# Step 1's first conv block added in pairs, and step 0's second product with two copies and two subtractions in other places

## The chip, the core and the metric

The kernel runs on one NeuronCore of a Trainium2 chip. The metric is the device time of one execution in microseconds; the number to compare is the median of several runs. The engines have their own instruction queues and meet by semaphores: TensorE (PE in the profile) multiplies, VectorE (DVE), ScalarE (ACT) and GpSimd (POOL) work on tiles in SBUF and PSUM, and SyncE (SP) issues transfers. GpSimd issues transfers as well, among them those that add to their destination (accumulates).

## The reference

`x` has 8 batches of 4096 positions with 192 channels; the channels form 8 heads with 7 weights each.

```python
w = exp(weight - max(weight))              # per head, over the 7 taps
w = w / (sum(w) + 1e-9)
x_pad = 6 rows of zeros in front of x
conv[b, s, channel] = sum over k of w[head, k] * x_pad[b, s + k, channel]

x = conv.reshape(32768, 192)
h = x @ w_in                               # 192 x 2048
g = h * (1.0 / (1.0 + np.exp(-1.702 * h)))
out = g @ w_out                            # 2048 x 192
```

Everything is float32.

## The kernel before, in words

The 32768 positions are worked in 32 steps (`N_BIG`, numbered from 0). A step takes a stretch of positions of two parts (n = 0, 1), has the convolution in three blocks of channels (c = 0, 1, 2), multiplies by `w_in` (the first product, line 599), applies the activation (ScalarE, lines 616 and 621), and multiplies by `w_out` (the second product, line 1045; in step 0 lines 845 and 850). Both products use schemes that replace some block products by sums of blocks. VectorE and GpSimd form those sums (`add_up`, lines 360 and 362). VectorE and ScalarE combine the product terms in PSUM banks (`sum2`, line 640; `copy2`, line 634).

Nothing reorders the instructions: each engine runs its queue in the order in which the program lists them. The steps from 2 on follow one list. Steps 0 and 1 are special, because step 0's weights and inputs are just arriving. The order around the change is written out in `first_step`, and in the generator `second_first`, which holds step 0's second product. That product works with two-by-two blocks: weights a11 to a22, activations b11 to b22, sums s1 to s4 and t1, t2, each in two halves [0] and [1]. The products go to four PSUM banks: `c11`, `a`, `c12`, `c21`. `go` issues matmuls in the rows 0 to 95 of a bank (line 845), and beside each group one that belongs to another bank's rest (`side`, line 850), whose result ScalarE copies away (line 852).

The bank `a` is used for three sums in a row, a11·b11, then + s2·t2, then + s3·b12, and each intermediate value is copied or added elsewhere before the next matmuls add to the bank. Line 890 copies the first value to `p1`, line 903 the second into the bank `c12`, and line 909 the second, later value into `c21`. Line 883 forms t2[1] = b22 − t1[1]; lines 906 and 913 later overwrite t2[0] and t2[1] with b21 − t2, which the product into `c21` uses. The values leave the banks by additions (907, 915, 943) and by transposes (961).

While step 0's second product runs, step 1's convolution is finished. Block c = 1 is made by VectorE (lines 474 and 476, `conv`). Blocks c = 2 and c = 0 are made by taps: ScalarE multiplies by one weight each (line 490, `tap`), the first into the block's own place, the other six into separate places, and the seven are added by accumulating transfers which GpSimd issues (line 513, `add_taps`). The list `TREE_1` gives the order of these additions: (1,2), (3,4), (0,1), (5,6), (0,3), (0,5), where (a,b) adds tap b to tap a. Each transfer moves 128 x 512 elements, 256 KB.

When all seven taps of c = 0 are in place and VectorE's convs are done, `need("done 1")` makes the first block sum (`OPEN_SUM`, the first L360 behind the convs). Behind it come the transfers that copy blocks between the halves of the partitions (`cross`, line 527), the other block sums (`next_sum`), the sums of `w_in` for the later scheme (`next_w`), and step 1's first product. In GpSimd's queue the accumulates are followed by the transfers of `add_forms` (line 409), whose other copies are on ScalarE (405 and 407).

Results of the first product are kept in PSUM banks and in places in SBUF called rooms (`room`); `ROOM_OF` says which value k0 to k9 goes to which room.

Of the kernel before, what the change touches and what calls it, by code (L numbers as in the profile page):

```python
# [15 lines left out]
def kernel(  # L16
# [289 lines left out]
    def split_piece(i, part=slice(0, PIECE)):  # L306

        split_e(i, part)
        split_m(i, part)

# [71 lines left out]
    def round_w_out(i):  # L382
        join_piece(NW + i)
        sign_piece(NW + i)
# [15 lines left out]
        round_piece(NW + i, dsts)  # L400
# [83 lines left out]
    TREE_1 = {2: [(1, 2)], 4: [(3, 4), (0, 1)], 6: [(5, 6), (0, 3), (0, 5)]}  # L484

    def tap(big, c, k):
# [11 lines left out]
        for a, b in (TREE if big > 1 else TREE_1).get(k, ()):  # L498
            tree.append((homes[a], homes[b]))
# [10 lines left out]
    def add_taps():  # L510
        if tree:
            out, src = tree.pop(0)
            nc.gpsimd.dma_start(out=out, in_=src, accum_op=ALU.add)  # L513

# [132 lines left out]
    FIRST = [  # L647
# [12 lines left out]
    ]  # L660
    ROOM_OF = ((4, 0, 3, 2, 1, 1, 0, 1, 1, 2), (0, 1, 4, 2, 3, 3, 2, 3, 3, 2))

    FILL = [
        {
            0: (("tap",), ("tap",), ("tap",), ("tap",), ("add", 4)), 2: (("add", 4), ("turn", 0)), 12: (("add", 4),),
            16: (("turn", 1),), 40: (("turn", 2),),
        },
        {
            0: (("vsum",),), 4: (("g", 0),), 7: (("vsum",), ("vsum",), ("vsum",), ("vsum",)), 10: (("vsum",),),
            13: (("g", 1),), 15: (("g", 2),), 17: (("g", 3),), 18: (("vsum",),), 20: (("vsum",),), 22: (("vsum",),),  # L670
            26: (("g", 4),), 32: (("vsum",),), 40: (("cross",),), 42: (("cross",),),
        },
    ]
    FILL_1 = [
        {
            0: (("tap",),), 3: (("add", 12), ("tap",), ("work", 0.8)), 4: (("work", 0.8),), 13: (("work", 0.8),),
            15: (("work", 0.8),), 16: (("tap",),), 23: (("tap",),), 31: (("tap",),),
        },
        {
            4: (("form", 2),), 5: (("g", 0), ("work", 0.8)), 9: (("g", 1),), 10: (("work", 0.8),),  # L680
            11: (("form", 3),), 14: (("turn", 0),), 17: (("turn", 1),), 19: (("turn", 2),), 20: (("g", 2),),
            25: (("g", 3),), 31: (("work", 0.8),), 32: (("g", 4), ("forms",)),
        },
    ]

    COUNT = {}
    for item in FIRST:
        for name in {s for s in item[2:] if isinstance(s, str) and s[0] == "a"}:
# [6 lines left out]
    def do(big, v, half, kind, *args):  # L695
# [7 lines left out]
        def at(name):  # L703
            return where[name] if name[0] == "a" else rooms[ROOM_OF[v][int(name[1:])]]
# [22 lines left out]
    later = []  # L727

    def seeds_ahead(big, half):

        while later and later[0][0] == "copy":
            dst = later[0][1]
            if dst[0] == "a" and dst not in half[0] and not free:
                return
            do(big, 0, half, *later.pop(0))

    def rest_ahead(big, half):
        while later:
            do(big, 0, half, *later.pop(0))

    def plain(u, m, n, v, slot, ks=range(NC), first=0):

        for k in ks:
            product1(slot, NC * (2 * u + m) + k, 2 * k + n, 0, v, k == first)

    def fill(big, kind, *args):
        if kind == "work":
            work(*args)
# [11 lines left out]
        elif kind == "form":  # L760
            add_forms(*args)
        elif kind == "turn":
# [8 lines left out]
    def hidden(big, v, now, nxt):  # L771

        for i, (ahead, *item) in enumerate(FIRST):
            for what in (FILL if big > 1 else FILL_1)[v].get(i, ()):
                fill(big, *what)
            if not ahead:
                do(big, v, now, *item)
            elif v == 0:
                do(big, 1, nxt, *item)
            elif nxt and ahead == 2:  # L780
                do(big + 1, 0, nxt, *item)
            elif nxt:
                later.append(item)
# [3 lines left out]

    def second_first(between, fetch, last_seeds):

        n3 = NC * Q  # L790
        groups = ((0, 2), (3, 1))

        def four(t, pi):
            return t.rearrange("p (v q h) e -> p v q h e", v=2, h=2)[:, :, pi, :, :]

        def place4(t):
            return t.rearrange("p (v h e) -> p v h e", v=2, h=2)

        pairs = g.rearrange("p (v q) n o (s h) t -> p v q n o s (h t)", v=2, s=2)

        def rows4(n, pi):
            return pairs[:, :, pi // 2, n, :, pi % 2, :]

        ws = [w_out_s[:, m, :, :] for m in range(2)]
        a11, a12, a21, a22 = ([four(t, pi[j]) for pi in groups] for t in ws for j in range(2))
        b11, b12, b21, b22 = ([rows4(n, pi[j]) for pi in groups] for j in range(2) for n in range(2))
        w4, t4 = NG * HD, NG * TOK
        room0 = conv_t[:, AT_X + NV - 5 : AT_X + NV, :].rearrange("p b t -> p (b t)")
        old0 = own(0).rearrange("p b t -> p (b t)")
        t1 = [place4(flat_room[:, 0:t4]), place4(places[:, 0:t4])]  # L810
        t2 = [place4(flat_room[:, t4 : 2 * t4]), place4(osbs)]
        s1, s2, s3, s4 = (
            [place4(flat[:, i * w4 : (i + 1) * w4]) for flat, i in two]
            for two in (
                ((flat_form, FORMS - 2), (old0, 0)), ((flat_form, FORMS - 1), (old0, 1)),
                ((room0, 0), (old0, 2)), ((old0, 3), (room0, 1)),
            )
        )
        p5, q12 = (flat_room[0:n3, 2 * t4 + i * TOK : 2 * t4 + (i + 1) * TOK] for i in range(2))
        p1 = room0[0:n3, 3 * T : 3 * T + TOK]  # L820
        assert 2 * w4 <= 3 * T and 4 * w4 <= NBLK * T and t4 <= (NA - 4 * NC) * UW
        add, sub = vec.tensor_add, vec.tensor_sub
        js = slice(0, TOK // Q)

        c11, a, c12, c21 = (slots[i][h] for h in range(2) for i in range(2))
        side = []

        def listed(w, t, gs=(0, 1)):
            return [
                (w[i][:, v, h, :], t[i][:, v, :, h * T : (h + 1) * T])  # L830
                for i in gs for v in range(2) for h in range(2)
            ]

        def aside(banks, *stages):

            for steps, to, start in stages:
                for c, bank in enumerate(banks):
                    for i, (w, t) in enumerate(steps):
                        last = to is not None and i == len(steps) - 1
                        side.append((bank[n3:, :], w[:, chunk_cols(c)], t, start and i == 0, last and chunk(to, c)))  # L840

        def go(bank, steps, first=True, more=False):
            for i, (w, t) in enumerate(steps):
# [553 lines left out]
```

## Time and profile before

| | us |
|---|---|
| three runs | 2267.24, 2268.92, 2269.05 |
| median | 2268.92 |
| profiled execution: span | 2266.2 |
| its time with TensorE busy | 2248.7 |
| with VectorE busy | 1981.8 |
| with ScalarE busy | 1708.1 |
| with GpSimd busy | 1067.6 |

The profile describes one execution on the core; for this one its span is the time that is known, and the runs' median stands 2.7 us above it. The steps from 2 on take the bulk of the span; the changed part lies between about 60 and 108 us from the start of the span, where the second product of step 0 and the first of step 1 meet. In the views a row gives the start, the busy time, the engine, the line of the kernel, the operation, what it writes and reads, the shape and the number of instructions taken together (x4). A bracket at the end gives the idle time in front of it and what ended it. The rows of stretches give for each engine the busy time and the number of instructions, then the granted TensorE clock, the share of the DMA engines, and GB/s.

### The profile page before, as it was taken

To read this page: it belongs to the slowest core of one execution; us is meant where nothing else is said; L and a number is where in the kernel's file an instruction comes from. 1 tells how busy PE (TensorE), PEld (TensorE's weight loads), DVE (VectorE), ACT (ScalarE), POOL (GpSimd) and SP (SyncE) were. 2 spreads that over 40 slices of the span, in tenths; PEclk is the share of its full clock that TensorE was granted. 3 is DMA by queue.
4 is the path that set the end of the run, shared out by engine and by line. 5 is a ranking of instruction groups with operands and counts; after the bars stand their busy time and mean duration, and the time that the engine had idled before them with its cause. 6 is when DMAs were issued, how large, how long until landed. Compare 5 with 4: busy or idle time off the path is not lost.

```text
span 2266.2 us, 62138 instructions
## 1 busy us (share of the span) xinstructions
PE 2248.7 (99%) x24966; PEld 1544.9 (68%) x24966; DVE 1981.8 (87%) x2967; ACT 1708.1 (75%) x3233; POOL 1067.6 (47%) x1101
## 2 busy tenths in 40 slices
PE   9999999999999999999999999999999999999999
PEld 5356577766777767777667776677776666766775
DVE  8898888988889888898888898888988888888888
ACT  8577877778777778777787777777777877777754
POOL 1455543555544555435554445554355544455510
PEclk9999999999999999999999999999999999999999
DMA  8986658666577666676665776666766657665543
GB/s 198 162 167 131 126 117 162 137 125 127 114 146 150 128 130 123 120 161 135 129 124 115 148 146 128 130 119 126 161 130 128 124 111 157 141 127 106 101 96 71
DMA packets 276111, 298.84 MB, mean 132 GB/s; under 512 B 119152, under 2 KB 203376, under 8 KB 275824
## 3 DMA queue, kind: packets, MB, share of 16 engines
q0 software_dynamic: 58080, 151.48, 37.2%
q1 hardware_dynamic: 216096, 142.99, 27.9%
q8 instruction: 198, 3.24, 0.6%
q14 instruction: 89, 0.73, 0.1%
q10 hardware_dynamic: 1648, 0.39, 0.1%
HBM read 53.15 MB, written 25.17 MB: 35 GB/s over the span
## 4 chain that ended last, share of the span: by engine, by line
PE 93%; DVE 4%; DMA 2%; ACT 1%; issue 1%; SPq 0%; POOL 0%; DVEq 0%; POOLq 0%; ACTq 0%
PE slot L599 48%; PE slot L1045 45%; DVE g L362 1%; DMA conv_t<-conv_t 1%; DMA g<-osbs 0%; PE slot L845 0%; DMA xin<-in_x_dram 0%; DVE room L362 0%; DMA conv_t<-w_form 0%; DVE w_out_s L345 0%; DVE xt L445 0%; DVE conv_t L476 0%; DVE room L337 0%; DVE room L330 0%; DVE osbs L360 0%
## 5 line engine op out<-in xcount | busy, mean ns | idle before, releaser
L599 PE MATMUL slot<-conv_t,w_in_s 64*128 64x512 f32 x5152 | 1147.7, 595 | 3.5 <-DVE slot L640 1.1
L599 PEld LDWEIGHTS slot<-conv_t,w_in_s 64*128 64x128 f32 x5152 | 661.2, 187 | 477.1 <-issue 321.8
L1045 PE MATMUL slot<-g,w_form 128*32 128x256 f32 x9672 | 894.3, 379 | 0.7 <-DVE room L362 0.7
L1045 PEld LDWEIGHTS slot<-g,w_form 128*32 128x32 f32 x9672 | 574.5, 110 | 127.8 <-DVE room L362 2.4
L508 POOL TENSOR_TENSOR conv_t<-conv_t,g 128x512 f32<-128x512 f32 x354 | 448.6, 1274 | 92.1 <-ACT g L490 60.5
L1045 PE MATMUL slot<-g,w_out_s 128*32 128x256 f32 x5952 | 467.3, 379 | 0.7 <-DVE g L362 0.7
L362 DVE TENSOR_TENSOR g<-g 128x1024 f32<-128x1024 f32 x372 | 450.9, 1224 | 8.5 <-DMA g<-osbs 1.9
L1070 ACT COPY room<-slot 32x256 f32<-32x256 f32 x651 | 237.6, 365 | 289.3 <-PE slot L1045 281.6
L640 DVE TENSOR_TENSOR room<-slot,room 128x512 f32<-128x512 f32 x620 | 383.6, 679 | 69.5 <-PE slot L599 69.5
L634 ACT COPY room<-slot 128x512 f32<-128x512 f32 x620 | 337.5, 595 | 75.0 <-PE slot L599 59.5
L490 ACT ACTIVATE g<-xt,cw 128x512 f32<-128x512 f32 x534 | 353.9, 715 | 3.6
L621 ACT ACTIVATE g<-room 128x1024 f32<-128x1024 f32 x248 | 265.7, 1071 | 78.2 <-DVE room L640 48.7
L616 ACT ACTIVATE g<-slot 128x512 f32<-128x512 f32 x528 | 282.3, 609 | 54.6 <-PE slot L599 35.6
L1021 POOL DMA_DIRECT2D g<-g x124 | 128.5, 1041 | 351.9 <-PE slot L1045 326.0
L640 DVE TENSOR_TENSOR slot<-slot,room 128x512 f32<-128x512 f32 x372 | 239.6, 689 | 54.5 <-PE slot L599 53.3
L1045 PEld LDWEIGHTS slot<-g,w_out_s 128*32 128x32 f32 x5952 | 239.8, 110 | 47.2 <-DVE room L640 22.0
L360 POOL TENSOR_TENSOR conv_t<-conv_t 128x256 f32<-128x256 f32 x210 | 181.9, 873 | 128.4 <-PE slot L599 119.1
L1045 PE MATMUL slot<-osbs,w_form 128*32 128x256 f32 x2232 | 229.2, 379 | 0.0
L513 POOL DMA_DIRECT2D g<-g x120 | 106.9, 891 | 240.6 <-ACT g L490 93.6
L1045 PEld LDWEIGHTS slot<-osbs,w_form 128*32 128x32 f32 x2232 | 131.8, 110 | 24.0
L640 DVE TENSOR_TENSOR slot<-room,slot 128x512 f32<-128x512 f32 x124 | 79.8, 687 | 42.4 <-PE slot L599 42.4
L1045 PE MATMUL slot<-room,w_form 128*32 128x256 f32 x1488 | 112.9, 379 | 0.2 <-DVE room L362 0.2
(170 smaller groups left out, 1658.8 us busy)
## 6 DMA issues: line engine op xcount, KB each, us to landing
g<-g POOLq DMA_DIRECT2D x124, 512.0 KB, 6.5
xin<-in_x_dram SPq DMA_DIRECT2D x240, 180.0 KB, 4.1
conv_t<-conv_t SPq DMA_DIRECT2D x186, 192.0 KB, 5.5
g<-g POOLq DMA_DIRECT2D x120, 256.0 KB, 5.5
conv_t<-conv_t SPq DMA_DIRECT2D x186, 128.0 KB, 2.9
out_dram<-osbs SPq DMA_DIRECT2D x186, 128.0 KB, 2.8
g<-room POOLq DMA_DIRECT2D x31, 512.0 KB, 5.0
conv_t<-g POOLq DMA_DIRECT2D x60, 256.0 KB, 5.2
```

Source lines behind the costliest of these rows:

```text
L360: eng.tensor_add(v(dst), v(a), v(b))
L362: eng.tensor_sub(v(dst), v(a), v(b))
L490: act.mul(home, conv_src(big, c, k), cw[:, c, k : k + 1])
L508: nc.gpsimd.tensor_add(dst, dst, home)
L599: nc.tensor.matmul(slot[h], w_in_s[halves[h], a, v * P : (v + 1) * P], src, start=first, stop=True, skip_group_check=True,)
L616: act.activation(dst[:, :, h, :], src[h].rearrange("p (o t) -> p o t", o=2), AF.Gelu_apprx_sigmoid, scale=float(sign),)
L621: act.activation(dst.rearrange("p o h t -> p h o t"), src.rearrange("p h (o t) -> p h o t", o=2), AF.Gelu_apprx_sigmoid, scale=float(sign),)
L634: act.copy(bank(dst, h), bank(src, h))
L640: op(*(bank(t, h) for t in (dst, a, b)))
L1021: nc.gpsimd.dma_start(out=spot(dst), in_=spot(a), accum_op=ALU.add)
L1045: nc.tensor.matmul(dst, w, t, start=first, stop=last, skip_group_check=True)
L1070: act.copy(to, d)
```

## The change

The text is largely rewritten: the planner with its costs (`work`) and the lists by index (`FIRST`, `FILL`, `FILL_1`) are replaced by two explicit lists in order, `OPENING` for step 0 and 1 and `ORDER` for the steps from 2 on. The order of TensorE's matmuls and of SyncE's transfers is the same, and so is every queue's from step 2 on. What differs in the instructions of steps 0 and 1:

1. In block c = 0 of step 1 the transfers add only (1,2), (3,4) and (5,6). The additions (0,1), (0,3), (0,5) are VectorE additions (`add_pair`), placed behind line 883 and ahead of the four convs and `need("done 1")`.
2. The two subtractions of lines 906 and 913 stand directly behind the block sums that follow the product s2·t2, with t2[1] first.
3. The copy to `p1` (890) stands ahead of the eight form copies, the copy to `c12` (903) ahead of one of the copies of line 852.
4. In step 1 the room of k0 and those of k1 and k6 are exchanged for v = 0 (`ROOM_1`).

```diff
-    TREE_1 = {2: [(1, 2)], 4: [(3, 4), (0, 1)], 6: [(5, 6), (0, 3), (0, 5)]}
+    TREE_1 = {2: {2: [(1, 2)], 4: [(3, 4), (0, 1)], 6: [(5, 6), (0, 3), (0, 5)]}, 0: {2: [(1, 2)], 4: [(3, 4)], 6: [(5, 6)]}}
...
+    def add_pair(c, a, b):
+
+        dst = own(1)[:, 2 * c : 2 * c + 2, :]
+        homes = [dst] + [tap_home(1, c, i) for i in range(1, K)]
+        vec.tensor_add(homes[a], homes[a], homes[b])
...
     ROOM_OF = ((4, 0, 3, 2, 1, 1, 0, 1, 1, 2), (0, 1, 4, 2, 3, 3, 2, 3, 3, 2))
...
+    ROOM_1 = ((0, 4, 3, 2, 1, 1, 4, 1, 1, 2), (0, 1, 4, 2, 3, 3, 2, 3, 3, 2))
...
-        add_forms(0)
-        go(a, listed(a11, b11))
-        sub(s3[1], a11[1], a21[1])
-        sub(s2[1], s1[1], a11[1])
-        sub(t2[1], b22[1], t1[1])
-        need("done 1")
...
-        act.copy(p1, whole(a))
-        sub(s4[0], a12[0], s2[0])
...
-        go(c11, p2[6:], first=False)
-        next_w(3)
-        act.copy(whole(c12), whole(a))
-        next_sum()
-        go(a, listed(s3, b12), first=False)
-        sub(t2[0], b21[0], t2[0])
-        add(p1, p1, whole(c11))
-        next_w(1)
-        act.copy(whole(c21), whole(a))
-        next_w(2)
-        next_sum()
-        next_w(1)
-        sub(t2[1], b21[1], t2[1])
...
+        ("w", "-", "s3", 0, "a11", "a21"), ("w", "+", "s1", 1, "a21", "a22"), ("go", "a", "a11 b11", 0, 8, 1, 0),
+        ("out", "p1", "a"), ("form", 0), ("w", "-", "s3", 1, "a11", "a21"), ("w", "-", "s2", 1, "s1", "a11"),
+        ("g", "-", "t2", 1, "b22", "t1"), ("pair", 0, 0, 1), ("pair", 0, 0, 3), ("pair", 0, 0, 5), ("done1",),
+        ("vsum",), ("w", "-", "s4", 0, "a12", "s2"), ("vsum",), ("go", "c11", "a12 b21", 0, 6, 1, 1), ("vsum",),
+        ("vsum",), ("vsum",), ("w", "-", "s4", 1, "a12", "s2"), ("vsum",), ("go", "a", "s2 t2", 0, 8, 0, 0),
+        ("vsum",), ("vsum",), ("out", "c12", "a"), ("g", "-", "t2", 1, "b21", "t2"), ("g", "-", "t2", 0, "b21", "t2"),
+        ("go", "c11", "a12 b21", 6, 8, 0, 0), ("w_in",), ("w_in",), ("w_in",), ("vsum",),
+        ("go", "a", "s3 b12", 0, 8, 0, 0), ("add", "p1", "c11"), ("w_in",), ("out", "c21", "a"), ("w_in",), ("w_in",),
...
+    halves_1 = [begin_half() for _ in range(3)]
+    first_step()
```

In the new list `("out", x, y)` is a ScalarE copy, `("g" ...)` and `("w" ...)` are VectorE additions and subtractions, `("go", bank, product, i, j, ...)` issues matmuls, `("vsum",)` is one block sum and `("w_in",)` one sum of `w_in`.

More of the change, by code (lines that the diff above doesn't have):

```diff
@@ L660 @@
     ]
+    SEED_AHEAD = ("copy", "k8", "a3", 1)
     ROOM_OF = ((4, 0, 3, 2, 1, 1, 0, 1, 1, 2), (0, 1, 4, 2, 3, 3, 2, 3, 3, 2))
[L663 to L673, printed above, removed]
@@ L725, in do @@
                 free.append(where.pop(n))
[L727 to L744, printed above, removed]
     def fill(big, kind, *args):
-        if kind == "work":
-            work(*args)
+        if kind == "conv":
+            next_conv()
         elif kind == "tap":
@@ L769, in fill, with first_products @@
             sum_g(*(EARLY_G if big > 1 else EARLY_G_1)[args[0]])
[L771 to L783, printed above, removed]
+    def first_products(big, halves, order):
+        for what, *item in order:
+            if isinstance(what, str):
+                fill(big, what, *item)
+            elif halves[what]:
+                do(big + what // 2, what % 2, halves[what], *item)
@@ L1106, with next_conv @@
     todo, ready = [], []
-    def work(us):
-        while todo and todo[0][1] <= us + 0.2:
-            us -= todo[0][1]
+    def next_conv():
+        if todo and todo[0][1]:
             todo.pop(0)[2]()
@@ L1320, in begin @@
+        free.extend((slots[2], sums, slots[0], slots[1]))
+        for item in OPENING:
+            ops[item[0]](*item[1:])
+        assert not side and not w_left
     def begin(big):
@@ L1322, in begin @@
         ready.extend(prepare_taps(big))
[L1324 to L1339 removed]
+    halves_1 = [begin_half() for _ in range(3)]
+    first_step()
+    half = halves_1[2]
     for big in range(1, N_BIG):
         more = big + 1 < N_BIG
[L1342 to L1349 removed]
+        if big > 1:
+            ahead = begin_half() if more else None
+            first_products(big, (half, begin_half(), ahead), ORDER)
+            half = ahead
         if more:
[L1351 to L1353 removed]
             cross_blocks(big + 1)
```

517 lines of the change are left out of this document (202 added, 315 removed), and 72 rows, old and new, of tables (FIRST, OPENING, ORDER, PLAN).

## The prediction

> **What bounds the kernel now.** I read the page first, then the chain of waits from 50 to 145 us, and then the timelines of VectorE, TensorE, ScalarE and GpSimd between 60 and 108 us, where the changed instructions lie.
>
> ```profile
> span 2266.2 us, 62138 instructions
> PE 2248.7 (99%) x24966; PEld 1544.9 (68%) x24966; DVE 1981.8 (87%) x2967; ACT 1708.1 (75%) x3233; POOL 1067.6 (47%) x1101
> PE 93%; DVE 4%; DMA 2%; ACT 1%; issue 1%; SPq 0%; POOL 0%; DVEq 0%; POOLq 0%; ACTq 0%
> ```
>
> TensorE is busy for 99% of the span and holds 93% of the chain, and the change takes no matmul away. Only time in which TensorE waits can be won. So I ask where the chain leaves TensorE near the change:
>
> ```profile
> 63.34 4.31 DMA conv_t<-conv_t
> ...
> 67.94 3.31 DMA conv_t<-conv_t
> ...
> 71.53 3.97 DMA conv_t<-conv_t
> ...
> 76.03 3.36 DMA conv_t<-conv_t
> ...
> 79.49 0.43 DVE conv_t L360
> ...
> 89.89 2.29 DVE osbs L913
> ...
> 92.32 0.63 PE slot L845 x3
> ...
> 102.02 0.59 ACT room L634
> 102.66 30.38 PE slot L599 x131
> ```
>
> Four accumulating transfers of step 1's first conv block follow one another; VectorE starts its block sum when the last has landed, works through its list up to the subtraction L913, and releases the product into c21 at 92.32. From 102.66 on TensorE runs by itself. What is won before 102.66 is therefore won at the end, as long as the waits that follow stay where they are.
>
> **The change, part by part.** The rest of the text is a rewriting of lists: the order of matmuls and of SyncE's transfers is the same, and from step 2 on every queue has its old order. Five things move.
>
> *The pairs.* Three of the six accumulates leave GpSimd's queue: (0,1), (0,3), (0,5). VectorE gets three adds of 128x512 in their place, behind L883 and ahead of the four convs L476.
>
> ```profile
> 68.03 2.28 DVE L883 TENSOR_TENSOR osbs<-g,w_in_s 128x2048 f32<-128x2048 f32 x1
> 70.23 3.11 DVE L476 SCALAR_TENSOR_TENSOR conv_t<-xt,cw,conv_t 128x512 f32<-128x512 f32 x4
> 79.49 0.42 DVE L360 TENSOR_TENSOR conv_t<-conv_t 128x256 f32<-128x256 f32 x1 [6.15 <-DMA conv_t<-conv_t]
> 79.95 0.42 DVE L362 TENSOR_TENSOR conv_t<-conv_t 128x256 f32<-128x256 f32 x1
> ...
> 83.27 0.76 DVE L362 TENSOR_TENSOR conv_t<-conv_t 128x256 f32<-128x256 f32 x2
> ...
> 85.41 2.28 DVE L906 TENSOR_TENSOR room<-g,room 128x2048 f32<-128x2048 f32 x1
> ...
> 89.89 2.28 DVE L913 TENSOR_TENSOR osbs<-g,osbs 128x2048 f32<-128x2048 f32 x1
> ...
> 101.34 0.68 DVE L943 TENSOR_TENSOR room<-room,slot 96x512 f32<-96x512 f32 x1
> ```
>
> An add of 512 elements isn't there in this form. From 0.42 for 256 and 2.28 for 2048 a straight line gives 0.69; L943, with one operand in PSUM, took 0.68. I take 0.69. Each add writes the operand of the next, so they don't overlap: the dependent pair 79.49 and 79.95 stands 0.04 beyond its busy time, which makes 3 x 0.69 less the usual overlap about 2.05. The convs then run from 72.3 to 75.4, and the block sum starts at 75.4. The idle 6.15 is gone and 2.05 is added: VectorE moves by −4.1 us. From below, the adds can't be under 3 x 0.42; from above, at 2.28 each (a row four times their size) the gain is nil.
>
> That holds if the transfers are there in time. GpSimd's rows:
>
> ```profile
> 63.34 2.09 POOL L513 DMA_DIRECT2D conv_t<-conv_t  x2
> 67.94 1.74 POOL L513 DMA_DIRECT2D conv_t<-conv_t  x2 [2.51 <-DMA conv_t<-conv_t]
> ...
> 76.03 0.86 POOL L513 DMA_DIRECT2D conv_t<-conv_t  x1 [3.64 <-DMA conv_t<-conv_t]
> 76.57 5.62 POOL L409 DMA_DIRECT2D w_form<-w_out_s  x6
> ```
> ```profile
> 79.49:105.88 26.39, 22.33 (x167) 7.11 (x169) 26.18 (x53) 13.65 (x25) 13.64 (x15) 1.00 1.09 195
> ```
>
> (1,2) and (3,4) were issued at 63.34 and about 0.54 later (76.03 to 76.57 is the same step). Now (5,6) follows at about 64.4 instead of waiting for 67.94. At the 195 GB/s of the loaded stretch in the last row 256 KB take 1.34 us, so behind (1,2), which took 4.31 and landed at 67.65, they land at about 69.0 and 70.3. The third add wants (5,6) at 71.6: 1.3 us of slack. Past that, lateness costs VectorE one for one.
>
> *Form transfers.* GpSimd's eight L409, behind the accumulates in its queue, start near 65 instead of 76.57. They take load from the stretch where the DMA share is 1.09; nothing near 65 waits behind them but themselves. Cost: nothing; if they held up (5,6), see the last rival.
>
> *The copies p1 and c12* on ScalarE:
>
> ```profile
> 68.75 0.56 ACT L890 COPY conv_t<-slot 96x512 f32<-96x512 f32 x1
> ...
> 78.22 0.58 ACT L852 COPY room<-slot 32x512 f32<-32x512 f32 x1 [2.85 <-PE slot L850]
> 78.82 0.56 ACT L903 COPY slot<-slot 96x512 f32<-96x512 f32 x1
> ...
> 104.24 1.19 ACT L634 COPY room<-slot 128x512 f32<-128x512 f32 x2 [0.53 <-DVE room L640]
> ```
> ```profile
> 67.82 0.61 PE L845 MATMUL slot<-g,w_out_s 128*32 128x512 f32 x3
> ...
> 69.36 0.63 PE L845 MATMUL slot<-room,w_form 128*32 128x512 f32 x3
> ...
> 79.44 1.06 PE L845 MATMUL slot<-g,conv_t 128*32 128x512 f32 x6 [1.28 <-ACT slot L903]
> 80.89 0.62 PE L850 MATMUL slot<-g,conv_t 128*32 128x512 f32 x1 [0.40 <-DVE conv_t L891]
> ...
> 88.22 0.60 PE L845 MATMUL slot<-g,conv_t 128*32 128x512 f32 x3
> 88.64 1.02 PE L850 MATMUL slot<-g,conv_t 128*32 128x512 f32 x2
> 92.32 0.63 PE L845 MATMUL slot<-osbs,w_out_s 128*32 128x512 f32 x3 [2.66 <-DVE osbs L913]
> 102.66 5.90 PE L599 MATMUL slot<-conv_t,w_in_s 64*128 64x512 f32 x25 [1.01 <-ACT room L634]
> ```
>
> Main matmuls come at a pitch of 0.43 (88.22 to 88.64). Without p1 behind the forms, the group of 69.36 could start at 68.25: 1.1. Its sixteen passes and the four of c11 end at 76.8, where s3·b12 can start instead of 79.44, since c12 no longer stands behind the side copy of 78.22: 1.5 more. L891 (s4[0]), which released the matmul of 80.89, moves with VectorE to about 76.7 and takes that pause with it: 0.6 (80.89 instead of 79.44 + 2 x 0.43). ScalarE's form copies, which p1 now precedes, feed only the form transfers above; L903 stood behind 2.85 of idle time and a side copy, so a copy of 0.56 ahead of them finds room.
>
> *The two subtractions.* L913 moves ahead of L906, both directly behind the sums that follow s4[1]. In before these end at 84.0 (83.27 + 0.76); less 4.1, L913 runs from 79.9 to 82.2 and L906 to 84.4. Twenty passes from 76.8 end at 85.4, where c21 starts without a wait instead of 92.32: 92.32 less 88.65 gives 3.7, and with the other three terms 6.9 in all. The order of VectorE's rows behind them is the old one, so the sum of its work stays: nothing is saved on VectorE beyond the 4.1.
>
> *Rooms.* k0, k1 and k6 of step 1 change places; one wait of VectorE goes, and no other is added. Nothing.
>
> **What of 6.9 reaches the end.** VectorE is busy for 26.18 of the 26.39 us after 79.49 (row above): it has no slack to give. TensorE's first products of step 1 need its results: the add L943, then the sums k0 (L640), then ScalarE's copy k4 at 104.24, which stood 0.53 behind L640. With TensorE 6.9 early and VectorE 4.1, the waits come back in small pieces where these are read, some 2.5 us between 97 and 101.5. The k4 copy ends at 105.43; the matmuls that overwrite its bank are the eighth pair from 102.66, at some 105.8 (seven pitches of 0.43 and a little), that is with 0.4 us to spare, since TensorE stood behind another copy at 102.66. So TensorE ends up ahead by 4.1 + 0.4 = 4.5. Behind that its list and its inputs move together. The span goes from 2266.2 to 2261.7. The three runs of before are 2267.24, 2268.92 and 2269.05; their median is 2.7 above the span of the profiled execution, so −4.5 on the median is **2264.4**.
>
> **The clock.**
>
> ```profile
> 134.80:138.20 3.40, 2.09 (x6) 0.99 (x8) 3.40 (x6) 2.91 (x6) 3.17 (x4) 1.00 0.53 119
> 138.20:141.60 3.40, 3.40 (x10) 2.34 (x9) 2.46 (x3) 0.37 (x1) 2.44 (x3) 0.50 1.17 246
> 90.40:93.80 3.40, 1.48 (x16) 0.50 (x16) 3.40 (x4) 0.25 (x1) 2.46 (x3) 1.00 1.03 200
> ```
>
> After a stretch of 3.4 us in which TensorE worked 2.09, the granted clock was 0.50 for 3.4 us; that cost half of it, 1.7. After one with 1.48 it stayed at 1.00. A pause alone doesn't decide. The spread of the three runs (1.8) is of that size. The Trainium skill ("TensorE: Matmul & The Clock Gate", Part 1) has half clock only after a whole idle window of about 3.4 us; this trace disagrees, with 2.09 us of work in the stretch ahead of the drop. By that rule the new pauses would cost nothing, and the forecast would stand.
>
> **The rivals.**
>
> *TensorE keeps the whole 6.9, or loses the half clock near 138.* For the first speaks that the waits on VectorE's sums are short; against it, that VectorE is full. 2268.9 − 6.9 = 2262.0. For the second, the pauses near 135 only have to fall otherwise on the clock's stretches: 2264.4 − 1.7 = 2262.7.
>
> *One more half clock.* The 2.5 us of pauses between 97 and 101.5 could be enough, as at 134.8: 2264.4 + 1.7 = 2266.1. Against it stands the row of 90.40.
>
> *The change does little.* If GpSimd's issue of (5,6) at 64.4 is held until L883 ends at 70.3, it lands 3.3 to 4.3 later (the chain's rows), at 74.6, and the third add waits 3.0: −1.5, 2267.4. For it speaks that the two issues at 63.34 took 2.09, where one took 0.86 at 76.03. [...]
>
> *Slower.* If the engines mix the eight form transfers (192 KB each, at 195 GB/s 8.1 us together) with (5,6), it lands at 70.3 + 8.1 = 78.4; the sum then starts at 82.2 instead of 79.49, and as TensorE's early start is worth 0.4 at most, the end is 2.3 later: 2271.2. It decides from a landing at 75.7 on, and passes 0.2% at about 80.6. Against it: the accumulate of 76.03 landed after 3.36, with six form transfers issued right behind it.
>
> **How the numbers follow.** Forecast 0.44; the two faster ends together 0.22; one more half clock 0.15; little 0.09; slower than before 0.10, as landing times under load may spread past the 8.1. A measurement of this kernel tells 0.2% (4.5 us) from no change, so faster begins at 2264.4, in the middle of the forecast: of its 0.44 I count 0.28 as faster, because the rounded steps (2.05 for the adds, 0.4 of slack) were rounded against the gain, and with the 0.22 that makes 0.50. Slower than 2273.4 needs a landing past 80.6: 0.08 of the last 0.10. The rest, 0.42, is within. The range from 2261.5 to 2268.0 takes in the two faster ends, the forecast, one more half clock and the mild form of "little".
>
> **What would show it.** Right: VectorE's row L360 near 75.4 without a wait on DMA; three adds of about 0.69 near 70.2; L913 near 80; c21's first matmul near 85.4; L599 running through from about 98 with short waits on L943, L640 and L634; and the whole tail 4.5 earlier. Wrong: an add waiting for a transfer, L360 later than 76, a wait ahead of c21 on L913 or L903, or a stretch of clock 0.50 before 110. The prediction fails on its sum if the tail's shift differs from VectorE's by more than 1 us.

## The result, and the profile after

| | us |
|---|---|
| changed kernel, median of 15 runs | 2262.55 (2261.78 to 2263.51) |
| kernel before, 15 runs, three of them those of the prediction | 2266.27 (2265.09 to 2269.05) |
| ratio, 95% interval | 0.9979 (0.9972 to 0.9987) |
| profiled execution, span | 2261.1, before 2266.2 |

The median of the changed kernel is 3.7 us lower, 0.16%. The ratio in the table is not the quotient of the two medians above it: 0.9979 is a gain of 0.21%, 4.8 us, and its interval takes in the 0.9984 of the medians. The forecast was 2264.4 with a gain of 4.5; the time lies 1.9 below it, near the fast end of the range from 2261.5 to 2268.0. The kernel before spreads over 4.0 us, the changed one over 1.7, and the median of before depends on how its runs fall: in four later comparisons, with 15 to 31 runs each, it was 2268.0 to 2268.3, and the changed kernel, run again, 2262.51, ratio 0.9976 (0.9967 to 0.9985). By medians the gain so lies between 3.7 and 5.8 us. The span of the profiled execution is 5.1 shorter; the time of a run stands 1.7 above its span here (2262.78 for the span of 2261.1).

The changed text has other line numbers: 355 and 357 are the sums (360 and 362 before), 469 the convs (476), 512 the pairs, 506 the accumulates (513), 402 the form transfers (409), 501 GpSimd's additions (508), 598 the first product (599), 633 and 639 its copies and sums (634 and 640), 855 the later second product (1045), 1115 and 1120 the matmuls of step 0's second product (845 and 850), 1134 its sums and subtractions, 1190 the copies p1, c12 and c21 (890, 903, 909).

The page, and VectorE's timeline of the changed kernel (start, busy time, engine, line, operation, shape, count):

```profile
span 2261.1 us, 62136 instructions
PE 2248.2 (99%) x24966; PEld 1552.0 (69%) x24966; DVE 1985.3 (88%) x2970; ACT 1707.7 (76%) x3233; POOL 1063.9 (47%) x1098
```
```profile
70.43 2.14 DVE L512 TENSOR_TENSOR conv_t<-conv_t 128x512 f32<-128x512 f32 x3
72.48 3.11 DVE L469 SCALAR_TENSOR_TENSOR conv_t<-xt,cw,conv_t 128x512 f32<-128x512 f32 x4
75.63 0.42 DVE L355 TENSOR_TENSOR conv_t<-conv_t 128x256 f32<-128x256 f32 x1
...
80.08 2.28 DVE L1134 TENSOR_TENSOR osbs<-g,osbs 128x2048 f32<-128x2048 f32 x1
...
99.64 1.24 DVE L639 TENSOR_TENSOR room<-slot,room 128x512 f32<-128x512 f32 x2
...
108.01 3.74 DVE L469 SCALAR_TENSOR_TENSOR conv_t<-xt,cw,conv_t 128x512 f32<-128x512 f32 x2
```

The three adds take 2.05 from start to the convs' start, none of them waits for a transfer, and the block sum starts at 75.63 instead of 79.49. The row of 108.01 is the new thing: two convs that took 1.53 before now take 3.74. TensorE, GpSimd and ScalarE of the changed kernel:

```profile
68.44 0.60 PE L1115 MATMUL slot<-room,w_form 128*32 128x512 f32 x3
...
77.02 0.60 PE L1115 MATMUL slot<-g,conv_t 128*32 128x512 f32 x3
...
85.60 0.61 PE L1115 MATMUL slot<-osbs,w_out_s 128*32 128x512 f32 x3
...
96.75 3.55 PE L598 MATMUL slot<-conv_t,w_in_s 64*128 64x512 f32 x12 [0.79 <-ACT room L633]
101.01 3.44 PE L598 MATMUL slot<-conv_t,w_in_s 64*128 64x512 f32 x13 [0.72 <-ACT room L633]
...
132.00 4.29 PE L598 MATMUL slot<-conv_t,w_in_s 64*128 64x512 f32 x16 [1.07 <-DVE slot L639]
```
```profile
64.13 2.97 POOL L506 DMA_DIRECT2D conv_t<-conv_t  x3
...
107.76 9.17 POOL L501 TENSOR_TENSOR conv_t<-conv_t,g 128x512 f32<-128x512 f32 x6
```
```profile
89.67 3.77 ACT L483 ACTIVATE g<-xt,cw 128x512 f32<-128x512 f32 x6
```

The pauses in step 0's second product are gone: s2·t2 starts at 68.44 (before 69.36), s3·b12 at 77.02 (79.44), c21 at 85.60 (92.32). Of c21's 6.7 the waits of 96.75 and 101.01 (on ScalarE's copies k8 and k4) and what lies between them take back 2.3. GpSimd's first addition starts at 107.76. The rows of before at the same places:

```profile
112.23 1.53 DVE L476 SCALAR_TENSOR_TENSOR conv_t<-xt,cw,conv_t 128x512 f32<-128x512 f32 x2
```
```profile
114.94 5.82 POOL L508 TENSOR_TENSOR conv_t<-conv_t,g 128x512 f32<-128x512 f32 x4
```
```profile
95.53 3.77 ACT L490 ACTIVATE g<-xt,cw 128x512 f32<-128x512 f32 x6
```
```profile
135.20 1.72 PE L599 MATMUL slot<-conv_t,w_in_s 64*128 64x512 f32 x4 [0.83 <-DVE slot L640]
137.83 4.63 PE L599 MATMUL slot<-conv_t,w_in_s 64*128 64x512 f32 x12 [0.92 <-ACT w_form L413]
```

Before, GpSimd's additions started 1.2 us after the convs were done. They have moved 7.2 us forward, the convs 4.2, and now they overlap. The chain of waits of the changed kernel leaves TensorE there, for the sum which stands behind the two convs in VectorE's queue:

```profile
111.67 0.69 DVE slot L639
...
112.41 1.72 PE slot L598 x5
```

The last sixteen matmuls of step 1's first product (4 and 12 before, 16 after) are a mark that every kernel here has: they start at 135.20 before and at 132.00 after, 3.2 us earlier. They end at 142.46 before (137.83 + 4.63, at half clock) and at 136.29 after. In this pair of profiles the half-clock stretch and the wait on L413 bring the larger part of what the span shows beyond 3.2; a wait of 0.5 that only the changed kernel has behind the mark takes a part of it back.

### The profile page after: what moved, and what is told of

The parts are those of the page before. It is cut to its first block, busy times and chain, and to the rows that moved or that the text cites. A ratio compares the mean times of both kernels' runs of the same rounds, so it can differ in the third digit from the quotient of the medians.

```text
span 2261.1 us, 62136 instructions
## 1 busy us (share of the span) xinstructions
PE 2248.2 (99%) x24966; PEld 1552.0 (69%) x24966; DVE 1985.3 (88%) x2970; ACT 1707.7 (76%) x3233; POOL 1063.9 (47%) x1098
## 4 chain that ended last, share of the span: by engine, by line
PE 96%; DVE 2%; ACT 1%; issue 1%; DMA 1%; POOL 0%; DVEq 0%; ACTq 0%; POOLq 0%; SPq 0%
PE slot L598 49%; PE slot L855 45%; PE slot L1120 1%; DVE g L357 1%; DMA g<-osbs 0%; PE slot L1115 0%; DVE room L357 0%; ACT g L615 0%; PE slot L946 0%; DVE room L639 0%; ACT w_form L483 0%; DMA xin<-in_x_dram 0%; DVE slot L639 0%; DVE room L355 0%; DVE osbs L771 0%
```

## The experiments

Three questions were open: which part of the change carries the gain, what the row of 108.01 costs and whence it comes, and whether the half-clock stretch belongs to the kernel before. In the lists of the changed kernel `("conv",)` and `("fill", "conv")` are one conv of VectorE, `("tap",)` one tap of ScalarE, `("turn", ...)` one of VectorE's transposes, `("do", 0, "sum", ...)` and `("do", 0, "copy", ...)` a sum of VectorE and a copy of ScalarE in step 1's first product. A `...` stands where lines, or parts of a line, are left out. Where the text says "matched one by one", the start of every matmul was compared with that of the same matmul in the other profile.

**The pairs alone.** The kernel before, with the tree cut and three additions.

```diff
         sub(t2[1], b22[1], t1[1])
+        add_pair(0, 0, 1)
+        add_pair(0, 0, 3)
+        add_pair(0, 0, 5)
         need("done 1")
```

> The kernel before with the first conv block's pairs alone: three accumulates less, three VectorE additions more, both copies and both subtractions at their old places. If VectorE sets the end (the forecast's reading), nearly all of the gain is here: VectorE's block sum starts 4.1 us earlier, c21 starts 4.1 earlier, and the end moves by -3 to -4.1 us (-1 of it lost again at 111 us if GpSimd's first additions collide with VectorE's convs there as in the changed kernel). If TensorE's own waits set the end, the waits on p1, c12 and t2 are still there and the end moves by under 2 us. A half-clock stretch more or less is 1.7 us on top of either.

Measured: 2262.94 (2261.48 to 2264.14), ratio to before 0.9977 (0.9968 to 0.9985), within 0.4 us of the changed kernel. VectorE's and GpSimd's timelines (its convs are line 476, its additions 508):

```profile
108.84 1.53 DVE L476 SCALAR_TENSOR_TENSOR conv_t<-xt,cw,conv_t 128x512 f32<-128x512 f32 x2
```
```profile
110.36 8.51 POOL L508 TENSOR_TENSOR conv_t<-conv_t,g 128x512 f32<-128x512 f32 x6
```

The pairs alone bring as much as the whole change, and here GpSimd starts at the moment when the convs end: no collision.

**The moves alone.** The changed kernel with six transfers again.

```diff
-... 0: {2: [(1, 2)], 4: [(3, 4)], 6: [(5, 6)]}}
+... 0: {2: [(1, 2)], 4: [(3, 4), (0, 1)], 6: [(5, 6), (0, 3), (0, 5)]}}
...
-        ("g", "-", "t2", 1, "b22", "t1"), ("pair", 0, 0, 1), ("pair", 0, 0, 3), ("pair", 0, 0, 5), ("done1",),
+        ("g", "-", "t2", 1, "b22", "t1"), ("done1",),
```

> The changed kernel with the first conv block again added by six transfers, so that only the two copies, the two subtractions and the rooms are moved. If VectorE sets the end: c21 starts some 5 us earlier than before, but the sums k0 and the copy k4 stay where they were, so the end moves by 0 to -0.4 us. If TensorE's waits set the end: -3 us or more.

Measured: 2265.85 (2265.02 to 2267.62) beside 2268.34 of before; ratio 0.9994 (0.9985 to 1.0003). The interval takes in no change, and leaves room for a gain of up to 3.4 us. The single times speak for some gain: ten of the eleven lie below 2266.8, and 22 of the 31 of the kernel before lie above 2267. The block sum and TensorE:

```profile
78.98 0.42 DVE L355 TENSOR_TENSOR conv_t<-conv_t 128x256 f32<-128x256 f32 x1 [5.59 <-DMA conv_t<-conv_t]
```
```profile
134.23 1.72 PE L598 MATMUL slot<-conv_t,w_in_s 64*128 64x512 f32 x4 [0.82 <-DVE slot L639]
136.86 2.94 PE L598 MATMUL slot<-conv_t,w_in_s 64*128 64x512 f32 x12 [0.91 <-ACT w_form L406]
```

The mark stands 1.0 earlier than before, of which 0.5 was there already at the block sum (78.98 instead of 79.49). The same wait of 0.9 stands ahead of the twelve, but they run at full clock: 2.94 instead of 4.63. That puts the price of this half-clock stretch at 1.7, and matched one by one TensorE keeps it to the end (the kernel before is 1.0 behind at the mark, 2.7 at 143 us and 2.6 at the last matmul).

**The copies and subtractions back, the pairs kept.** The changed kernel's list, with the two `("out", ...)` and the two `("g", ..., "t2", ...)` at the places of before.

```diff
-        ("out", "p1", "a"), ("form", 0), ...
+        ("form", 0), ...
...
+        ("vsum",), ("out", "p1", "a"), ("w", "-", "s4", 0, "a12", "s2"), ...
...
-        ... ("out", "c12", "a"), ("g", "-", "t2", 1, "b21", "t2"), ("g", "-", "t2", 0, "b21", "t2"),
...
+        ... ("w_in",), ("w_in",), ("w_in",), ("out", "c12", "a"), ("vsum",),
+        ... ("g", "-", "t2", 0, "b21", "t2"), ("add", "p1", "c11"), ...
+        ... ("g", "-", "t2", 1, "b21", "t2"), ("xt2", 0), ...
```

> The changed kernel with both copies and both subtractions at their old places, so that the pairs (and the rooms) are left. If the moves themselves cause the collision at 108 us (ScalarE's taps follow c21, c21 comes 6.5 us earlier, and so GpSimd's additions come 7 us earlier and meet VectorE's convs): GpSimd's first addition now starts behind the convs, near 110 us, the two convs take 1.5 us, c21 starts some 2.5 us later than in the changed kernel, and the end is 0.3 to 0.6 us earlier than there. If the moves carry part of the gain: up to 2 us later than the changed kernel.

Measured: 2262.53 (2261.72 to 2263.67): the changed kernel's time to 0.02 us.

```profile
108.46 1.53 DVE L469 SCALAR_TENSOR_TENSOR conv_t<-xt,cw,conv_t 128x512 f32<-128x512 f32 x2
```
```profile
110.41 8.53 POOL L501 TENSOR_TENSOR conv_t<-conv_t,g 128x512 f32<-128x512 f32 x6
```

The collision is gone with the moves, as expected, and the mark (131.25) is 0.75 earlier than in the changed kernel; but the runs don't show it. The 0.3 to 0.6 that I expected of them did not come. The mark itself differs by 0.4 between two profiles of the changed kernel (132.00 and 131.60). What the runs show is that on top of the pairs the moves bring nothing.

**Only the subtractions back.**

```diff
-        ... ("out", "c12", "a"), ("g", "-", "t2", 1, "b21", "t2"), ("g", "-", "t2", 0, "b21", "t2"),
+        ... ("out", "c12", "a"),
...
+        ... ("g", "-", "t2", 0, "b21", "t2"), ("add", "p1", "c11"), ...
+        ... ("g", "-", "t2", 1, "b21", "t2"), ("xt2", 0), ...
```

> The changed kernel with the two subtractions at their old places, the copies at their new ones. VectorE's work has the same sum, so its reading says: c21 starts about 2.5 us later, at 88, the sums k0 and the copy k4 do not move, the wait ahead of them gets shorter by as much, and the end is within 0.5 us of the changed kernel. If the subtractions carry a part of the gain: 1 to 2.5 us later.

Measured: 2262.63 (2261.67 to 2263.83), the same.

```profile
108.12 3.39 DVE L469 SCALAR_TENSOR_TENSOR conv_t<-xt,cw,conv_t 128x512 f32<-128x512 f32 x2
```
```profile
109.21 8.86 POOL L501 TENSOR_TENSOR conv_t<-conv_t,g 128x512 f32<-128x512 f32 x6
```
```profile
88.21 0.63 PE L1115 MATMUL slot<-osbs,w_out_s 128*32 128x512 f32 x3 [1.84 <-DVE osbs L1134]
...
132.08 5.99 PE L598 MATMUL slot<-conv_t,w_in_s 64*128 64x512 f32 x16 [1.38 <-DVE slot L639]
```

c21 is 2.6 us later than in the changed kernel, and the mark at 132.08 instead of 132.00. TensorE's lead at c21 was worth nothing at the mark. Its profile had a half-clock stretch in the sixteen (5.99 instead of 4.29). The two stretches on either side of the drop, with busy times by engine, then the granted clock, DMA share and GB/s:

```profile
129.87:133.28 3.41, 2.04 (x8) 0.83 (x8) 3.41 (x4) 3.41 (x8) 3.25 (x4) 1.00 0.88 210
133.28:136.69 3.41, 3.41 (x11) 2.65 (x9) 3.41 (x5) 1.00 (x3) 1.21 (x1) 0.50 1.17 228
```

Here the half clock cost nothing in the end: matched one by one TensorE is 1.3 behind the changed kernel at 135.7 us, and 0.2 ahead of it at 159 us, because two short pauses of the changed kernel, of 0.50 ahead of 136.80 and of 0.81 at 153.2, are absent.

**The convs out of GpSimd's way.** The changed kernel, with the last two convs ahead of two sums.

```diff
-        ("do", 0, "prod", 1, "a1"), ("do", 0, "sum", "k3", "a4", "+", "k4"), ("do", 0, "sum", "k5", "a1", "-", "k1"),
-        ("fill", "conv"), ("do", 0, "prod", 18, "a2"), ("do", 0, "gelu", 1, 1, "a3", 1), ("fill", "conv"),
+        ("do", 0, "prod", 1, "a1"), ("fill", "conv"), ("fill", "conv"), ("do", 0, "sum", "k3", "a4", "+", "k4"), ...
+        ("do", 0, "prod", 18, "a2"), ("do", 0, "gelu", 1, 1, "a3", 1),
```

> The changed kernel with the last two convs of block 1 ahead of the sums k3 and k5 instead of behind them. If GpSimd's additions, which now start at 107.8 us, hold up VectorE's two convs (3.74 us for the two instead of 1.53), the convs now take 1.5 us, the wait of 1.1 us ahead of the matmuls at 112.4 is gone, and the end is 0.7 to 1.1 us earlier than in the changed kernel (about -4.5 against the kernel before). If the wait there has another cause, the end stays or is up to 0.5 us later, since the convs stand ahead of two sums with 1.0 us of idle time only.

Measured: 2261.97 (2261.44 to 2263.20), ratio to before 0.9973 (0.9963 to 0.9983); the changed kernel run beside it 2262.51.

```profile
104.45 1.53 DVE L469 SCALAR_TENSOR_TENSOR conv_t<-xt,cw,conv_t 128x512 f32<-128x512 f32 x2
```
```profile
131.00 4.30 PE L598 MATMUL slot<-conv_t,w_in_s 64*128 64x512 f32 x16 [1.06 <-DVE slot L639]
```

The convs take 1.53 again, and are over before GpSimd's additions begin at 107.08. The mark is 1.0 earlier than in the changed kernel; the median gained 0.5, less than the 0.7 to 1.1 expected, and its range overlaps that of the changed kernel. In the trace the collision is what cost TensorE its wait ahead of 112.4; in the time about half of that shows. Matched one by one, TensorE is 1.0 ahead of the changed kernel up to 185 us and 0.6 from 231 us on, so the other half is lost again behind step 1; the second profile of the changed kernel is itself 0.3 ahead of the first at the last matmul.

**The changed kernel again.**

> The changed kernel itself beside the others on the same chip: about -3.7 us, with the wait of about 1 us at 111 us and no stretch at clock 0.50 between 100 and 240 us if that belongs to the change; if the lost half-clock stretch is chance, it can be back, with 1.7 us more.

Measured: 2262.51 (2262.11 to 2263.69). The convs at 107.89 took 3.45, GpSimd's additions began at 107.35, the mark stands at 131.60, and the clock does not fall before 2259 us, behind the last matmul, as in the first profile.

**The kernel before again.**

> The kernel before as it is, for a second profile. If the half-clock stretch at 138 us in its first profile belongs to some executions only, the single times fall into two groups about 1.7 to 2.4 us apart, and a profile either has the stretch again at 138 us or ends about 1.7 us earlier. If it belongs to every execution, the times stand in one group.

Measured: 2268.76 (2265.98 to 2269.57) beside 2268.23 of before itself; the span of its profile is 2267.5. The single times do not fall into two clean groups: ten of these eleven lie between 2268.3 and 2269.6 and one at 2265.98, but the 29 beside them fill the stretch from 2265.4 to 2269.7. Two stretches of the profile, and two rows of VectorE and GpSimd:

```profile
89.60:93.01 3.41, 0.76 (x9) 0.23 (x11) 3.41 (x5) 1.27 (x4) 3.41 (x4) 1.00 1.08 223
93.01:96.42 3.41, 3.41 (x18) 0.94 (x12) 3.38 (x9) 0.59 (x2) 0.07 (x1) 0.50 1.12 201
```
```profile
114.09 4.21 DVE L476 SCALAR_TENSOR_TENSOR conv_t<-xt,cw,conv_t 128x512 f32<-128x512 f32 x2
```
```profile
114.31 5.12 POOL L508 TENSOR_TENSOR conv_t<-conv_t,g 128x512 f32<-128x512 f32 x3
```

The half-clock stretch is not at 138 now. It stands right behind the wait of 2.6 us ahead of c21, which the change removes. And the collision of convs and additions, absent from the first profile of before, is there in this one: the convs are 1.9 us later (114.09 instead of 112.23), the additions are not (114.31, there 114.94). So both occur in the kernel before in some executions, the half clock at more than one place.

**Two transposes late, one conv early.**

```diff
-        ("turn", 1, 1, "p5"), ("tap",), ...
+        ("tap",), ...
...
-        ... ("turn", 0, 1, "q12"), ("tap",), ("store", 0, 1),
+        ... ("tap",),
...
         ... ("do", 0, "sum", "a1", "a2", "-", "k0"),
+        ("turn", 1, 1, "p5"), ("turn", 0, 1, "q12"), ("store", 0, 1), ...
...
+        ... ("fill", "conv"), ("do", 0, "sum", "k3", "a4", "+", "k4"), ...
-        ... ("do", 0, "gelu", 1, 1, "a3", 1), ("fill", "conv"),
+        ... ("do", 0, "gelu", 1, 1, "a3", 1),
```

> The changed kernel with two of VectorE's transposes (of p5 and q12) behind the sums k0 and a1 instead of ahead of them, and one of the two convs of the collision ahead of the sums k3 and k5. If the sum k0 and the copy k4 behind VectorE's full stretch are what holds TensorE back at 101 us: these come 1.3 us earlier and TensorE with them, the collision costs at most half, and the end is 1.0 to 2.0 us earlier than in the changed kernel. If TensorE is held by something else at 96 to 101 us, the end moves by under 0.5 us.

Measured: 2260.98 (2260.60 to 2261.79), ratio to before 0.9971 (0.9960 to 0.9982), and 1.5 us under the changed kernel; the two ranges only touch.

```profile
98.27 1.25 DVE L639 TENSOR_TENSOR room<-slot,room 128x512 f32<-128x512 f32 x2
...
107.30 2.50 DVE L469 SCALAR_TENSOR_TENSOR conv_t<-xt,cw,conv_t 128x512 f32<-128x512 f32 x1
```
```profile
130.08 4.29 PE L598 MATMUL slot<-conv_t,w_in_s 64*128 64x512 f32 x16 [0.81 <-DVE slot L639]
```

The sum k0 comes 1.4 us earlier, the wait of 101.01 is not in TensorE's list of waits any more, and the mark is 1.9 earlier than in the changed kernel. This is the fastest kernel of the study. Its span of 2258.7 is 2.2 to 2.4 below that of the changed kernel, its median only 1.5: in this kernel and the four that follow a run's time stands 2.0 to 2.1 above its span instead of 1.7, and why is not known.

**The transposes alone.** As the kernel before this one, with both convs at the places of the changed kernel.

> The changed kernel with the two transposes behind the sums k0 and a1, both convs at their place behind k3 and k5. If the transposes carry the gain of the kernel that also moved one conv (-1.5 us against the changed kernel) through the sum k0 and the copy k4: VectorE's sum k0 starts near 98.3, TensorE is ahead by 5.5 us after it, and the end is 1.0 to 1.5 us earlier than in the changed kernel. If the moved conv carried it: under 0.5.

Measured: 2262.58 (2261.47 to 2263.80), no gain on the changed kernel.

```profile
107.36 4.15 DVE L469 SCALAR_TENSOR_TENSOR conv_t<-xt,cw,conv_t 128x512 f32<-128x512 f32 x2
```
```profile
112.17 6.27 PE L598 MATMUL slot<-conv_t,w_in_s 64*128 64x512 f32 x26 [0.50 <-DVE slot L639]
...
131.77 4.29 PE L598 MATMUL slot<-conv_t,w_in_s 64*128 64x512 f32 x16 [1.07 <-DVE slot L639]
```

My reading, that the transposes carried the gain, was wrong in this form. The sum k0 is early here too (98.33), but the convs then come to 107.36, at GpSimd's start, and take 4.15; TensorE waits, and the mark is back at 131.77. The earlier sums pay only where a conv is out of the collision as well.

**The transposes late, both convs early.** As the kernel with two transposes late, with the other conv early as well.

```diff
+        ... ("fill", "conv"), ("fill", "conv"), ("do", 0, "sum", "k3", "a4", "+", "k4"), ...
```

> The kernel with the turns late, and now both of the convs that met GpSimd's additions stand ahead of the sums k3 and k5. There one conv was left behind the sums; it took 2.50 us instead of 0.75 and TensorE lost 0.7. If that collision is the cause, no conv takes more than 0.8 us any more and the end comes 0.5 to 0.7 us earlier than with one of them left. If the sums k3 and k5, 0.7 us later on VectorE, then hold TensorE, nothing is gained.

Measured: 2261.73 (2261.44 to 2262.71), 0.75 slower than with one conv. No conv collides (1.53 for two), but the sums k3 and k5 start at 105.69 instead of 104.89, and the mark stands at 130.78 instead of 130.08. The second of the two theories holds: what a conv saves behind the sums it costs ahead of them.

**One accumulate back, the convs ahead of the adds.** As with the turns late, with (0,1) as a transfer behind (5,6).

```diff
-... 0: {2: [(1, 2)], 4: [(3, 4)], 6: [(5, 6)]}}
+... 0: {2: [(1, 2)], 4: [(3, 4)], 6: [(5, 6), (0, 1)]}}
...
-        ... ("pair", 0, 0, 1), ("pair", 0, 0, 3), ("pair", 0, 0, 5), ("done1",),
+        ... ("conv",), ("conv",), ("conv",), ("conv",), ("pair", 0, 0, 3), ("pair", 0, 0, 5), ("done1",),
```

> The kernel with the turns late, in which the addition (0,1) is again a transfer, issued behind (5,6), and the four convs of VectorE stand ahead of the two additions left. If VectorE sets the time up to the copy k4, its block sum starts 0.7 us earlier (75.0) and TensorE gains up to 0.5 us at 101 us, where it lost that much on k4. If the transfer (0,1) lands later than 73.5 us, the block sum waits for it, and the gain is lost one for one.

Measured: 2262.68 (2262.46 to 2263.85), 1.7 slower than without it.

```profile
73.85 1.42 DVE L512 TENSOR_TENSOR conv_t<-conv_t 128x512 f32<-128x512 f32 x2 [0.37 <-DMA conv_t<-conv_t]
```

The transfer landed near 73.8, so half of the 0.7 went into waiting for it. The mark (130.35) is within 0.3 of the kernel without this edit, yet the span is 2261.3 instead of 2258.7: over two microseconds are lost behind it, most of them in the steps from 2 on, whose order is the same. The list of TensorE's waits behind 240 us holds a single one of 0.5. Matched one by one, TensorE falls behind the kernel without this edit at four places: by 0.58 at 553 us, 0.29 between 1521 and 1529, 0.66 at 2081 and 0.30 at 2151, 1.8 in all, with the clock at 1.00. At each of them one VectorE sum with two inputs in SBUF takes longer, with GpSimd's additions beside it: 2.93 instead of 2.36, 1.70 instead of 1.40, 2.36 instead of 1.69, 1.98 instead of 1.69. No other VectorE instruction behind 250 us differs by more than 0.12. The first of the four, without the edit and with it, and TensorE behind it:

```profile
550.46 2.36 DVE L357 TENSOR_TENSOR osbs<-osbs,g 128x1024 f32<-128x1024 f32 x1
```
```profile
550.76 2.93 DVE L357 TENSOR_TENSOR osbs<-osbs,g 128x1024 f32<-128x1024 f32 x1
```
```profile
550.90 1.70 POOL L357 TENSOR_TENSOR conv_t<-conv_t 128x256 f32<-128x256 f32 x2
```
```profile
554.35 1.72 PE L598 MATMUL slot<-conv_t,w_in_s 64*128 64x512 f32 x4 [0.47 <-DVE slot L639]
```

So the collision of step 1 has relatives in the later steps, and a shift of tenths of a microsecond between VectorE and GpSimd decides what they cost. Why the two engines stand differently to each other there was not followed.

**All of them, and k8 ahead of a tap.** Turns late, both convs early, (0,1) by a transfer, and the copy k8 before a tap.

> Turns late, both convs early, (0,1) by a transfer, and ScalarE's copy k8 ahead of the tap that stood before it (0.72 us). If the ties found are the ones that count, TensorE's wait of 0.8 us on k8 at 96 us is gone as well and the end is 0.7 to 1.5 us earlier than with the turns late alone. If VectorE's full stretch takes it back, under 0.7.

Measured: 2263.41 (2262.66 to 2264.45), slower than the changed kernel by 0.9. The wait on k8 is gone from TensorE's list, as expected; the span is 2261.6, and it too loses in the later steps: the same four sums are long (2.92, 1.69, 2.37 and 1.98), and no others. With the last kernel it shares the fourth accumulate and the order of convs and adds, which the faster ones lack; that one of these shifts the engines was not tried.

## Why the prediction was right, point by point

*The pairs.* Right. Three adds, 2.05 us; the block sum at 75.63 where 75.4 was said. The profile stands 0.20 later where the adds begin (70.43, before 70.23), so VectorE moved by 3.86 + 0.20 = 4.06 where 4.1 was said. No add waited, so the slack of the third transfer was enough, and both rivals of late transfers fell: GpSimd's three issues, 64.13 to 67.10, were not held until VectorE's subtraction ended at 70.5.

*TensorE's four terms.* Right: 68.44, 77.02 and 85.60 where 68.25, 76.8 and 85.4 were said. Their worth at the end was called at most 0.4, and with the moves undone the time was the same. Alone, without the pairs, they may be worth more (the interval allows 3.4); that was not settled.

*VectorE's full stretch sets what reaches the end.* Right as a mechanism. TensorE's lead of 6.7 at c21 shrank to 4.4 when the wait on k4 was over, where 4.5 was said: matched one by one, the matmul that starts at 105.39 before is the one of 101.01 after. The pairs alone, the pairs without the moves and the full change give 2262.94, 2262.53 and 2262.55. Without the moves c21 starts 2.6 later than in the changed kernel, and behind the wait on k4, at 103 us, TensorE is 0.3 later: VectorE's list takes the lead back.

*"Behind that its list and its inputs move together."* This step failed. ScalarE's taps stand behind a copy that waits for the matmuls beside c21, and came 5.9 us earlier with it (89.67 instead of 95.53). GpSimd's accumulates follow the taps: in every profile the first starts 1.0 behind the start of the third tap. Its additions stand behind the last accumulate and came 7.2 earlier, while VectorE's convs came 4.2 earlier. Where they met, two convs took 2.2 us more, and TensorE's mark is 3.2 early instead of 4.4. The prediction had named a shift of the tail other than VectorE's by more than 1 us as what would break its sum: 3.2 at the mark and 5.1 in the span stand against 4.1, at the edge of that on either side. "From 102.66 on TensorE runs by itself" had also left out the waits of 0.83 and 0.92 ahead of 135.20 and 137.83. I had looked for what waits for the moved work, but not for what it would run beside.

*The clock.* The rival that the half clock near 138 goes took place in the profile, and it was given only a part of 0.22. Its price of 1.7 was right there (4.63 against 2.94 for the same twelve); with the subtractions back a stretch of the same length cost nothing in the end. That, and the wait on L413, gone too, made up for the collision: that a forecast of 4.5 lies within the 3.7 to 5.8 measured is in part luck. That the time came out 1.9 below the forecast is mostly the base, since the median 2268.92 of three runs was 2.65 above that of fifteen (and 0.6 to 0.9 above the later ones). The forecast's ratio, 0.9980, was nearer to the measured 0.9979 than its time. The extra half clock between 97 and 101.5 was not seen in any of the profiles with the change.

*Where the chances lay.* The bound of 0.2% fell within the interval of the ratio, as the prediction had it in the middle of its forecast.

## What to carry to other kernels

When a full engine gets slack, ask what of its lead the next engines can keep: TensorE had 6.7 us, and 4.4 of it stayed, because VectorE's list behind was full. When work moves forward on several engines by different amounts, look for pairs of instructions which share something and didn't overlap before; here two convs and GpSimd's additions. Undoing the collision alone gained 0.5, late transposes alone nothing, and late transposes with one conv moved 1.5. Such pairs of instructions can also cost something hundreds of microseconds later, where nothing was edited. And with gains of 0.2%, take the kernel before often: its median moved by 2 us between comparisons.

## What I had not expected of the hardware

VectorE's operations with two inputs in SBUF were held up when GpSimd's additions ran. Two convs took 3.74, 3.45, 3.39, 4.15 and 4.21 us where the additions began between 0.54 us ahead of their start and 1.1 us behind it, and 1.53 where they did not overlap (the kernel before in its first profile, the pairs alone, the moves undone, the convs early). A single conv took 2.50 instead of 0.75. Sums with one input in PSUM were not held up (0.68 each beside the additions, as elsewhere). Single instructions of the changed kernel, and the addition beside the single conv of 107.30 in the kernel with the turns late:

```profile
107.76 1.74 POOL L501 TENSOR_TENSOR conv_t<-conv_t,g 128x512 f32<-128x512 f32 x1
```
```profile
108.01 2.06 DVE L469 SCALAR_TENSOR_TENSOR conv_t<-xt,cw,conv_t 128x512 f32<-128x512 f32 x1
```
```profile
107.49 1.75 POOL L501 TENSOR_TENSOR conv_t<-conv_t,g 128x512 f32<-128x512 f32 x1
```

In the changed kernel the addition ends at 109.50 and the conv at 110.06 (rounded sums of the rows); with the turns late they end at 109.24 and 109.79. In all the profiles with the collision a held conv ends 0.54 to 0.56 behind the end of one addition. So it waits for a whole addition. The first of the six takes 1.74 to 1.76 with or without a conv beside it; the others take 1.26 to 1.28, and 1.60 to 1.62 where a held conv ends beside them. The Trainium skill ("SBUF — State Buffer", SBUF: two separate sides) says that a VectorE operation with two inputs in SBUF and a GpSimd operation that reads SBUF exclude each other: whichever of the two starts first has the shared ports for its whole instruction while the other is blocked. That one waits for the whole of the other agrees with these rows. Who goes first does not, by the starts that the profiles record: the conv of 107.30 starts 0.19 ahead of the addition and ends behind it, and three others that start 0.17 to 0.31 ahead do the same; no row shows when an instruction takes the ports.

Before the last step the granted clock fell to 0.50 in three of the profiles, twice in the kernel before and once in a variant (the subtractions back), each time for 3.41 us. In the 3.41 us ahead of these drops TensorE worked 2.12, 0.76 and 2.04 us. The same kernel had the drop at 138 us in one execution and at 93 us in another. What decides it beyond such a pause stayed open: in the first profile the stretch from 90.4 to 93.8, with 1.48 of 3.40 us worked, brought none, and neither did that from 133.4 to 136.8 in the moves alone, with 1.73.
